# Spectral filter and max-out MLP on one core: who doubles the filter in the opening, and evacuations of two PSUM banks

## Chip, cores, metric

The kernel runs on one core of a Trainium2 chip. The metric is the device time of one execution in microseconds (us). The engines are TensorE (matmul), VectorE, ScalarE, GpSimd and SyncE; in the profile they are PE (with PEld for weight loads), DVE, ACT, POOL and SP. Transfers are issued by SyncE (the hardware queue, q1) and by GpSimd (the software queue, q0).

## The reference

A batch of 8 sequences of 3072 tokens with 256 channels is filtered along the sequence in the frequency domain; the result, taken as 24576 tokens, goes through an MLP that takes the larger of two projections.

```python
X = np.fft.rfft(x, axis=1)                      # x: 8 x 3072 x 256
Y = X * (filt_r + 1j * filt_i)[None]            # filter: 1537 x 256
y = np.fft.irfft(Y, n=3072, axis=1).astype(np.float32)
t = y.reshape(24576, 256)
out = np.maximum(t @ w1, t @ w2) @ w_out        # w1, w2: 256 x 1024, w_out: 1024 x 256
```

## The kernel before

**Algorithm.** The length 3072 is split as 96 x 32, and the transforms are matmuls against tables that the kernel makes itself: `C1` (forward, 96 points), `U` (forward, 32 points with the twiddle factors), `VP` and `VQ` (the way back over 32 points), `G1` (back over 96 points). Between forward and back lies the product with the filter `F`. The max-out uses max(a, b) = b + relu(a - b): `Wd` is w1 - w2, `M` is w2 times w_out, and a token block is relu(y Wd) Wo + y M.

**Steps of a batch.** `s1` (or `f1`) multiplies x by the 96-point table; `s2` multiplies by `U` and leaves `px` in PSUM, two tiles for each `v` (s = 0, 1); `product` multiplies `px` by `F` into `pq`, real and imaginary filter at once (128 partitions x 1024 elements); `s3` multiplies by `VP` and `VQ`; `s4` makes the time signal from `zr`; `moe_h` and `moe_o` are the MLP. `v` runs over 6 groups, each of 2 of the 12 filter windows `w`. From the second batch on these steps are spread over 64 steps of the MLP of the batch before, by the lists at the end of the kernel. That steady loop takes up most of the time.

**The opening** is the first batch, which has no MLP beside it. It is written out by hand (L562 to L651), under a manual schedule: each engine runs its instructions in the order in which the code gives them. [...] `spin` issues matmuls on a constant whose result is not used.

**The filter.** `F` holds each value on two groups of 32 partitions (0 to 31 and 32 to 63, and the same from 64). `load_f` brings it from memory into the first of each with transfers of GpSimd that also convert to bfloat16: for windows 0 to 7 and then 8 to 11, and in each for two partition halves `g` and two parts `ri`, rows upward (L117) and rows backward (L120). `double_f` copies it to the second group: windows 0 to 7 by four VectorE copies (L130), windows 8 to 11 by four transfers of SyncE (L132), behind which SyncE issues the loads of w1 and w2 (L281, L282). `fix_f` sets one row.

**Who multiplies.** VectorE makes the s = 0 products of all six groups. The s = 1 products of groups 0, 2, 3 and 4 are GpSimd's (`POOLED`), that of group 1 VectorE's, and that of group 5 is shared, half and half (`shared_product`, L388 and L389). GpSimd's queue is: loads of x, the issues of `F`, a load of the second batch (`load_x(1, 0, 2)`, L172), its products, two further x loads, `Wd` first half, the load of `Wo`, an x load, `Wd` second half, `CT`.

**PSUM.** Two pools hold the 8 banks from the start: `ps` (6 tiles of one bank) and `pso` (2). A tile waits until the buffer it takes has been read.

**Order of rows.** `U`, `bt` and `zT` are indexed by `u = 2 * w + g` (w = 2v + i), and `kc` and `kap`, from which the tables come, count in that order.

Of the kernel before, what the change touches and what calls it, by code (L numbers as in the profile page):

```python
# [26 lines left out]
def kernel(  # L27
# [40 lines left out]
    ps = ctx.enter_context(tc.tile_pool(name="ps", bufs=6, space=bass.MemoryType.PSUM))  # L68
    pso = ctx.enter_context(tc.tile_pool(name="pso", bufs=2, space=bass.MemoryType.PSUM))
# [3 lines left out]
    pq0 = setup.enter_context(tc.tile_pool(name="pq0", bufs=6))  # L73
    ctx.enter_context(tc.manual_schedule())
# [35 lines left out]
    def load_f(h):  # L110
        w0, w1 = WP[h]
        n = 2 * (w1 - w0)
        for g in range(2):
            for ri, f in enumerate((filt_r, filt_i)):
                k0 = 24 * g + 2 * w0
                src = bass.AP(f.tensor, f.offset + k0 * D, [[96 * D, 16], [D, n], [1, D]])
                G.dma_start(out=F[64 * g:64 * g + 16, ri, w0:w1].rearrange("p w s d -> p (w s) d"), in_=src)  # L117
                n0 = 1 if k0 == 0 else 0
                src = bass.AP(f.tensor, f.offset + (96 - k0 - n0) * D, [[96 * D, 16], [-D, n - n0], [1, D]])
                G.dma_start(out=F[64 * g + 16:64 * g + 32, ri, w0:w1].rearrange("p w s d -> p (w s) d")[:, n0:n],  # L120
                            in_=src)
                if n0:
                    src = bass.AP(f.tensor, f.offset + 48 * D, [[96 * D, 16], [1, D]])
                    G.dma_start(out=F[16:32, ri, 0, 0], in_=src)

    def double_f(h, g, ri, engine):
        w0, w1 = WP[h]
        o_, i_ = F[64 * g + 32:64 * g + 64, ri, w0:w1], F[64 * g:64 * g + 32, ri, w0:w1]
        if engine is V:
            V.tensor_copy(o_, i_)  # L130
        else:
            nc.sync.dma_start(out=o_, in_=i_)  # L132
# [9 lines left out]

    V.memset(W1, 1.0)
# [3 lines left out]
    kc = init.tile([NP, NW, 2, 2], FP32)  # L147
    kap = init.tile([128, NW, 2], FP32)
# [3 lines left out]
    hv = init.tile([128, 2, 1], FP32)  # L152
    load_x(0, 0, 1)
    G.iota(pid, pattern=[[1, 1]], base=0, channel_multiplier=1, allow_small_or_imprecise_dtypes=True)
    G.iota(kc, pattern=[[2, NW], [24, 2], [1, 2]], base=0, channel_multiplier=0,
           allow_small_or_imprecise_dtypes=True)
    load_x(0, 1, 1)
    G.iota(kap, pattern=[[2, NW], [24, 2]], base=0, channel_multiplier=0,
# [4 lines left out]
    for c in range(3, 8):  # L163
        load_x(0, c, 1)
    for q in range(2):
        G.memset(hv[:, q], 1.0)
        for r in (0, 32):
            G.memset(hv[r:r + 1, q], 0.5 * (1 - q))
    load_f(0)
    load_f(1)  # L170
    load_fn()
    load_x(1, 0, 2)  # L172

    def table_c():
# [4 lines left out]
        kf = kc.rearrange("p w g s -> p (w g s)")  # L179
# [16 lines left out]
    def tables_u():  # L196
# [24 lines left out]
        V.tensor_scalar(t1[:, 0], kap.rearrange("p w g -> p (w g)"), a_, base, OP.mult, OP.add)  # L221
# [19 lines left out]
    def sines_u(h):  # L241
        uv = ua.rearrange("p u c s j -> p u (c s j)")
        S.activation(U[:, NW * h:NW * h + NW], uv[:, NW * h:NW * h + NW], AF.Sin, bias=zero, scale=TWO_PI)

    def table_g():
        pg = ps.tile([96, NP], FP32, tag="ps", name="pg")
# [3 lines left out]
    def table_v(h, q):  # L250
        pool, tag = (pso, "po") if h else (ps, "ps")
        pv = [pool.tile([128, 6, 64], FP32, tag=tag, name="pv%d" % s) for s in range(2)]
        for i in range(6):
            for g in range(2):
                for s in range(2):
                    rows = slice(64 * s, 64 * s + 64)
                    u = 2 * (6 * h + i) + g
                    if q == 0:
                        TE.matmul(pv[s][64 * g:64 * g + 64, i], U[rows, u], I128[rows, rows], start=True, stop=True)
                    else:  # L260
                        TE.matmul(pv[s][64 * g:64 * g + 32, i], U[rows, u, 32:64], I128[rows, rows],
                                  start=True, stop=True)
                        TE.matmul(pv[s][64 * g + 32:64 * g + 64, i], U[rows, u, 0:32], NI[rows, rows],
# [3 lines left out]
    def put_v(h, q, pv):  # L267
        for s in range(2):
            i0 = 1 if h == 0 and s == 0 else 0
            tab = VQ if q else VP  # L270
            if i0:
                S.activation(tab[:, 0, 0], pv[0][:, 0], AF.Identity, bias=zero, scale=hv[:, q])
            S.activation(tab[:, 6 * h + i0:6 * h + 6, s], pv[s][:, i0:6], AF.Copy)  # L273
# [97 lines left out]
    def s2(b, v):  # L371
        px = [ps.tile([128, 2, D], FP32, tag="ps", name="px%d" % s) for s in range(2)]
        for i in range(2):
            for s, g in ((0, 0), (1, 1), (0, 1), (1, 0)):
                u = 2 * (2 * v + i) + g
# [4 lines left out]
    def product(E, v, s, px, pool=None):  # L380
# [3 lines left out]
        return pq  # L384

    def shared_product(v, s, px, xs_, pool):
        pq = pool.tile([128, 2, 2, D], BF16, tag="pq", name="pq")
        V.tensor_tensor(pq[:, 0], px, F[:, 0, 2 * v:2 * v + 2, s], OP.mult)  # L388
        G.tensor_tensor(pq[:, 1], xs_, F[:, 1, 2 * v:2 * v + 2, s], OP.mult)  # L389
        return pq  # L390

    def s3(b, v, pq):
# [9 lines left out]
        for g in range(2):  # L402
            S.activation(zt[:, :, g], pz[g], AF.Copy)  # L403
        nc.sync.dma_start(out=zd[b][4 * v:4 * v + 4].rearrange("u p d -> p u d"),
                          in_=zt.rearrange("p i g d -> p (i g) d"))
# [89 lines left out]
    def s1t(c):  # L495
        for dc in range(2):
            pa = ps.tile([128, 4, 96], FP32, tag="ps", name="pa")
            for m in range(4):
                TE.matmul(pa[:, m], xb[0, c][:, m, 128 * dc:128 * dc + 128], C1, start=True, stop=True)
            o_ = at2[:, dc].rearrange("p u q m -> p (u q) m")[:, :, 4 * c:4 * c + 4]  # L500
            i_ = pa.rearrange("p m q -> p q m")
            if dc == 1 and c >= 6:
# [237 lines left out]
```

## Time and profile before

| what | value |
|---|---|
| median of 3 runs | 503.91 us (503.34 to 505.15) |
| the profiled execution's own time | 503.8 us |
| its span (first to last instruction) | 502.0 us |
| mean granted TensorE clock | 0.992 |
| TensorE busy | 488.4 us, 97% |
| VectorE, ScalarE, GpSimd busy | 331.9, 308.3, 257.5 us |
| four doublings on VectorE (L130) | 1217 ns each |
| ScalarE evacuations in `s1t` (L505) | 14 of 487 ns |
| products on VectorE and on GpSimd in the opening (L382) | 7 of 1217 ns, 4 of 2130 ns |

A row of a timeline gives the start in us from the span's start, the busy time, the engine, the line of the kernel, the operation, what it writes and reads, how many there are, and in brackets how long the engine stood idle before it and what ended that. The chain of waits is followed back from the last instruction to what released each piece. Issues of transfers are listed with size and time to landing, from the start of the issue.

### The profile page before, as it was taken

The page shows a single profiled execution, that of the slowest core. Times are in us where ns is not written, and L with a number is a line of the kernel's source. Part 1 is how long each engine was busy: PE and PEld are TensorE (multiplying, and loading weights), DVE is VectorE, ACT ScalarE, POOL GpSimd, SP SyncE. Part 2 cuts the span into 40 slices and gives each one's busy share as a digit, 9 for nine tenths or more (in the row PEclk, how much of TensorE's full clock was granted, in tenths as well). Part 3 has the DMA queues.
Part 4 walks back from the last instruction along what each step waited for, and adds up shares of the span by engine and source line. Part 5 has one row for each costly group of instructions (what it writes and reads, how often), then busy time and mean ns, then how long its engine had stood idle before and what let it go on. Part 6 is the DMA issues. An engine that isn't in the chain of part 4 may idle for free.

```text
span 502.0 us, 13079 instructions
## 1 busy us (share of the span) xinstructions
PE 488.4 (97%) x5299; PEld 362.1 (72%) x5303; DVE 331.9 (66%) x518; ACT 308.3 (61%) x629; POOL 257.5 (51%) x338
## 2 busy tenths in 40 slices
PE   8688999999999999999999999999999999999997
PEld 3455777777777777777777777777777777777775
DVE  7876688457865777457765687557765687555553
ACT  6776478647774676557764586647774465544442
POOL 7893569547463864645654855537632221222220
PEclk9989999999999999999999999999999999999999
DMA  7999789995799667986779558896769235411112
GB/s 125 150 252 217 230 229 290 306 274 171 212 268 260 175 204 234 250 229 189 198 244 275 187 177 245 235 239 197 197 181 255 78 111 153 168 65 64 64 64 84
DMA packets 77966, 97.20 MB, mean 194 GB/s; under 512 B 8017, under 2 KB 54354, under 8 KB 77842
## 3 DMA queue, kind: packets, MB, share of 16 engines
q1 hardware_dynamic: 64642, 66.73, 49.6%
q0 software_dynamic: 13264, 29.64, 20.3%
q8 instruction: 41, 0.67, 0.6%
q14 instruction: 19, 0.16, 0.1%
HBM read 53.87 MB, written 47.19 MB: 201 GB/s over the span
## 4 chain that ended last, share of the span: by engine, by line
PE 90%; DMA 5%; POOL 2%; issue 1%; ACT 1%; DVE 0%; SPq 0%; POOLq 0%; DVEq 0%
PE po L476 34%; PE ph L448 33%; PE po L474 8%; PE pz L399 5%; PE py L428 4%; PE pa L349 2%; DMA F<-in_filt_r_dram 2%; PE px L376 2%; DMA Wo<-in_moe_w_out_dram 2%; POOL xb L88 1%; DMA F<-F 1%; PE pr L549 1%; POOL pq L382 0%; PE pt L528 0%; PE pm__1132 L306 0%
## 5 line engine op out<-in xcount | busy, mean ns | idle before, releaser
L476 PE MATMUL po<-Wo,gt 128*128 128x256 bf16 x1536 | 261.0, 273 | 0.2 <-DMA Wo<-in_moe_w_out_dram 0.2
L452 ACT ACTIVATE gt<-ph 128x384 bf16<-128x384 f32 x321 | 157.0, 496 | 147.9 <-PE ph L448 147.3
L461 POOL DMA_DIRECT2D out_dram<-ot x186 | 102.6, 555 | 187.1 <-DVE ot L488 184.4
L476 PEld LDWEIGHTS <-gt 128*128 128x128 bf16 x1536 | 146.6, 98 | 66.1 <-issue 10.3
L450 DVE TENSOR_SCALAR gt<-ph 128x384 bf16<-128x384 f32 x191 | 104.9, 552 | 63.1 <-PE ph L448 59.9
L382 DVE TENSOR_TENSOR pq<-px,F 128x1024 bf16<-128x1024 f32 x91 | 107.0, 1219 | 24.2 <-PE px L376 22.6
L448 PEld LDWEIGHTS <-Wd 128*128 128x128 bf16 x1024 | 96.5, 98 | 12.9 <-POOL Wd L292 1.4
L103 POOL TENSOR_TENSOR xb<-XF 128x512 bf16<-128x512 f32 x48 | 61.2, 1276 | 41.3 <-DMA XF<-in_x_dram 21.2
L488 DVE COPY ot<-po 128x512 f32<-128x512 f32 x95 | 65.1, 685 | 25.3 <-PE po L476 25.0
L104 POOL TENSOR_TENSOR xb<-XF 128x512 bf16<-128x512 f32 x48 | 61.0, 1271 | 0.0
L403 ACT ACTIVATE zt<-pz 128x512 bf16<-128x512 f32 x84 | 45.6, 595 | 11.5 <-PE pz L399 8.4
L353 ACT ACTIVATE at<-pa 128x512 bf16<-128x512 f32 x96 | 51.8, 610 | 1.2 <-PE pa L349 0.8
L428 PE MATMUL py<-G,zr 96*128 96x96 bf16 x512 | 32.7, 206 | 0.2
L428 PEld LDWEIGHTS <-zr 96*128 96x128 bf16 x512 | 29.0, 97 | 2.5 <-DVE zr L552 0.4
L399 PE MATMUL pz<-pq,VP 64*64 64x256 bf16 x336 | 21.9, 281 | 0.0
L376 PE MATMUL px<-bt,U 64*64 64x256 bf16 x384 | 19.8, 278 | 1.2 <-ACT VQ L273 0.7
L399 PE MATMUL pz<-pq,VQ 64*64 64x256 bf16 x336 | 20.9, 269 | 0.0
L349 PE MATMUL pa<-xb,CT 64*64 64x512 bf16 x192 | 19.5, 383 | 0.0
L399 PEld LDWEIGHTS <-VP 64*64 64x64 bf16 x336 | 9.7, 105 | 13.3 <-issue 13.3
L376 PEld LDWEIGHTS <-U 64*64 64x64 bf16 x384 | 10.4, 109 | 3.9 <-issue 3.3
L559 PE MATMUL pd<-W 128*128 128x512 bf16 x30 | 10.5, 462 | 1.7 <-DVE zero L145 1.5
L552 DVE COPY zr<-pr 96x1024 bf16<-96x1024 bf16 (+1 forms) x8 | 5.2, 649 | 8.0 <-PE pr L549 8.0
(429 smaller groups left out, 609.7 us busy)
## 6 DMA issues: line engine op xcount, KB each, us to landing
out_dram<-ot POOLq DMA_DIRECT2D x186, 128.0 KB, 3.3
XF<-in_x_dram SPq DMA_DIRECT2D x96, 192.0 KB, 4.6
ad<-at SPq DMA_DIRECT2D x56, 192.0 KB, 3.3
bt<-ad SPq DMA_DIRECT2D x14, 768.0 KB, 9.1
zd<-zt SPq DMA_DIRECT2D x42, 256.0 KB, 2.7
zr<-zd SPq DMA_DIRECT2D x56, 192.0 KB, 4.8
WS<-in_moe_w_dram SPq DMA_DIRECT2D x4, 512.0 KB, 5.1
xb<-in_x_dram POOLq DMA_DIRECT2D x8, 192.0 KB, 5.8
```

What stands on the lines that cost most here:

```text
L103: G.tensor_tensor(t_[:, 0], f[:, 0], f[:, 1], OP.add)
L104: G.tensor_tensor(t_[:, 1], f[:, 0], f[:, 1], OP.subtract)
L353: S.activation(at[:, m0:m0 + 2], pa[g], AF.Copy)
L382: E.tensor_tensor(pq, px.rearrange("p (o i) d -> p o i d", o=1).to_broadcast([128, 2, 2, D]), F[:, :, 2 * v:2 * v + 2, s], OP.mult)
L399: TE.matmul(pz[g][64 * s:64 * s + 64, i], tab[64 * g:64 * g + 64, 2 * v + i, s], pq[s][64 * g:64 * g + 64, q, i], start=(q == 0), stop=(q ...
L428: TE.matmul(py[:, m], zr[b][:, 4 * i + m, 128 * dc:128 * dc + 128], G1, start=True, stop=True)
L448: TE.matmul(ph, Wd[:, dc, 128 * j:128 * j + 128], y_[:, dc], start=(dc == 0), stop=(dc == 1))
L450: V.tensor_scalar(gt[tt][:, j], ph, 0.0, None, OP.max)
L452: S.activation(gt[tt][:, j], ph, AF.Relu)
L461: E.dma_start(out=dst, in_=ot[tt // 2][:, 3 * (tt % 2) + c])
L476: TE.matmul(p_, g_[:, n - 2, blk], Wo[:, n - 2], start=(e == 0), stop=(e == 9))
L488: V.tensor_copy(ot[tt // 2][:, e - 1:e + 1], po[0])
```

## The change

- `double_f` works on three parts of four windows. VectorE copies windows 0 to 3 (groups v = 0, 1); SyncE copies windows 4 to 7 and then 8 to 11, eight transfers of the same size as the four before.
- `load_f` is called by direction: for windows 0 to 7 the four upward loads, then the backward ones, then the same for windows 8 to 11. The transfers are the same eighteen.
- Until the end of the opening, PSUM is held by `pair` (2 tiles of two banks) and `single` (4 tiles of one bank); `ps` and `pso` are opened after it. ScalarE evacuates both banks of a pair in one instruction: in `s1t` for c < 7, in `put_v`, and in `s3t` for v < 5. In the last call of `s1t` and of `s3t`, ScalarE and VectorE take one bank each.
- The order of rows becomes `u = 4 * v + 2 * g + i`; `kc`, `kap`, `s2`, `table_v`, `zT` and (in the steady loop too) the block order inside `zt` follow it.
- The factor 0.5 or 0 for the first row moves from an evacuation with a scale (L272) into `U0`, one VectorE multiplication with `hv`, for which GpSimd makes 3 memsets instead of 6.
- `sines_u(0)` follows c = 3 instead of 4, `sines_u(1)` follows the last `s1t`; `put_v`, `s2`, `products` and `s3t` are reordered; GpSimd gets the s = 1 products of groups 0 to 3, VectorE those of 4 and 5; `load_x(1, 0, 2)` is issued behind the first product; `s3t` has one constant matmul ahead for every v.

```diff
-    ps = ctx.enter_context(tc.tile_pool(name="ps", bufs=6, space=bass.MemoryType.PSUM))
-    pso = ctx.enter_context(tc.tile_pool(name="pso", bufs=2, space=bass.MemoryType.PSUM))
+    pair = setup.enter_context(tc.tile_pool(name="pair", bufs=2, space=bass.MemoryType.PSUM))
+    single = setup.enter_context(tc.tile_pool(name="single", bufs=4, space=bass.MemoryType.PSUM))
...
-    def load_f(h):
+    def load_f(h, sign):
...
+                r0 = 64 * g if sign > 0 else 64 * g + 16
+                o_ = F[r0:r0 + 16, ri, w0:w1].rearrange("p w s d -> p (w s) d")
+                if sign > 0:
+                    src = bass.AP(f.tensor, f.offset + k0 * D, [[96 * D, 16], [D, n], [1, D]])
+                    G.dma_start(out=o_, in_=src)
+                else:
+                    src = bass.AP(f.tensor, f.offset + (96 - k0 - n0) * D, [[96 * D, 16], [-D, n - n0], [1, D]])
+                    G.dma_start(out=o_[:, n0:n], in_=src)
...
     def double_f(h, g, ri, engine):
-        w0, w1 = WP[h]
-        o_, i_ = F[64 * g + 32:64 * g + 64, ri, w0:w1], F[64 * g:64 * g + 32, ri, w0:w1]
+        ws = slice(4 * h, 4 * h + 4)
+        o_, i_ = F[64 * g + 32:64 * g + 64, ri, ws], F[64 * g:64 * g + 32, ri, ws]
...
-    load_f(0)
-    load_f(1)
+    for h in range(2):
+        load_f(h, 1)
+        load_f(h, -1)
     load_fn()
-    load_x(1, 0, 2)
...
     def put_v(h, q, pv):
-        for s in range(2):
-            i0 = 1 if h == 0 and s == 0 else 0
-            tab = VQ if q else VP
-            if i0:
-                S.activation(tab[:, 0, 0], pv[0][:, 0], AF.Identity, bias=zero, scale=hv[:, q])
-            S.activation(tab[:, 6 * h + i0:6 * h + 6, s], pv[s][:, i0:6], AF.Copy)
+        S.activation((VQ if q else VP)[:, 6 * h:6 * h + 6].rearrange("p i s m -> p s i m"), pv, AF.Copy)
...
     def s1t(c):
+        pa = two("pa") if c < 7 else None
...
+        if c < 7:
+            S.activation(o_, pa.rearrange("p c m q -> p c q m"), AF.Copy)
+        else:
+            S.activation(o_[:, 0], pa[0].rearrange("p m q -> p q m"), AF.Copy)
+            V.tensor_copy(o_[:, 1], pa[1].rearrange("p m q -> p q m"))
...
     def s3t(v, pq):
...
+        zv = zT[:, :, :, 4 * v:4 * v + 4].rearrange("p c m u q -> p u (c m) q")
+        if v < 5:
+            S.activation(zv, t_.rearrange("p g (i q n) -> p (g i) n q", i=2, q=4), AF.Copy)
+        else:
+            S.activation(zv[:, 0:2], pz[0].rearrange("p i s r c m -> p i (c m) (s r)"), AF.Copy)
+            V.tensor_copy(zv[:, 2:4], pz[1].rearrange("p i s r c m -> p i (c m) (s r)"))
...
-    for g in range(2):
-        for ri in range(2):
-            double_f(1, g, ri, nc.sync)
+    for h in (1, 2):
+        for g in range(2):
+            for ri in range(2):
+                double_f(h, g, ri, nc.sync)
...
-    POOLED = (0, 2, 3, 4)
+    POOLED = (0, 1, 2, 3)
...
-    pxs = {v: s2(0, v) for v in (1, 0)}
-    stage_x(0)
...
+    pxs = {v: s2(0, v) for v in (0, 1)}
+    for v in range(2):
+        stage_x(v)
+    for q in range(2):
+        put_v(0, q, table_v(0, q))
+    for v in range(2):
+        pqs[v] = products(v)
+        if v == 0:
+            load_x(1, 0, 2)
+        pxs[v + 2] = s2(0, v + 2)
+        stage_x(v + 2)
+        put_v(1, v, table_v(1, v))
+    s3t(0, pqs[0])
+    pqs[2] = products(2)
+    pxs[4] = s2(0, 4)
+    pqs[3] = products(3)
     s3t(1, pqs[1])
...
     for v in (4, 5):
         pqs[v] = products(v)
-    for v in (4, 5):
+    for v in (2, 4, 3, 5):
         s3t(v, pqs[v])
...
+    ps = ctx.enter_context(tc.tile_pool(name="ps", bufs=6, space=bass.MemoryType.PSUM))
+    pso = ctx.enter_context(tc.tile_pool(name="pso", bufs=2, space=bass.MemoryType.PSUM))
```

## The prediction

> **What bounds the kernel now.** I read the page first: engines, 40 slices, chain. TensorE is busy 97% of the span and the chain is 90% TensorE; the rest of the chain (transfers, GpSimd, 10%) lies in the opening. The edits to the steady loop change the order of filter rows in `u` and the place of blocks inside `zt`, not one size or count, so I cost the loop at nothing: its instructions would keep their rows (84 evacuations of 595 ns at L403). The change can only move the moment from which TensorE is fed without a gap. That moment I looked up in the chain of waits in order of time (start, length, what):
>
> ```profile
> PE 90%; DMA 5%; POOL 2%; issue 1%; ACT 1%; DVE 0%; SPq 0%; POOLq 0%; DVEq 0%
> ...
> 16.69 4.13 DMA F<-in_filt_r_dram
> ...
> 21.61 3.23 DMA F<-F
> ...
> 30.64 2.10 POOL pq L382
> 32.73 1.15 POOL pq L389
> ...
> 37.19 9.41 DMA Wo<-in_moe_w_out_dram
> 46.60 0.04 issue
> 46.64 0.60 PE po L476 x4
> ```
>
> From 46.64 on it is TensorE nearly throughout. Before that it is the filter: loaded by GpSimd, doubled over the partitions, multiplied on GpSimd. The timelines of VectorE and GpSimd show how tightly these sit (start, busy, line, idle before):
>
> ```profile
> 18.15 1.22 DVE L130 COPY F<-F 32x4096 bf16<-32x4096 bf16 x1
> 19.40 0.28 DVE L140 CAST F<-FN 1x256 bf16<-1x256 f32 x1
> 19.72 3.60 DVE L130 COPY F<-F 32x4096 bf16<-32x4096 bf16 x3
> 23.82 5.75 DVE L382 TENSOR_TENSOR pq<-px,F 128x1024 bf16<-128x1024 f32 x5 [0.50 <-DVE F L130]
> 30.60 2.36 DVE L382 TENSOR_TENSOR pq<-px,F 128x1024 bf16<-128x1024 f32 x2 [1.03 <-DMA F<-F]
> 32.87 0.68 DVE L388 TENSOR_TENSOR pq<-px,F 128x512 bf16<-128x512 f32 x1
> ```
> ```profile
> 17.69 0.53 POOL L120 DMA_DIRECT2D F<-in_filt_i_dram  x1
> 18.22 1.25 POOL L117 DMA_DIRECT2D F<-in_filt_r_dram  x1
> 19.57 1.49 POOL L120 DMA_DIRECT2D F<-in_filt_r_dram  x1
> 21.05 1.24 POOL L117 DMA_DIRECT2D F<-in_filt_i_dram  x1
> 22.28 1.17 POOL L120 DMA_DIRECT2D F<-in_filt_i_dram  x1
> 23.43 0.52 POOL L88 DMA_DIRECT2D xb<-in_x_dram  x1
> ```
>
> Two things are to be seen. While VectorE runs its four copies, each filter issue on GpSimd takes 1.2 to 1.5 us instead of 0.5, one issue per copy, so the last leaves at 22.28. And VectorE then stands 1.03 us until 30.60 for SyncE's last transfer (issued 26.45, landed 30.45). After it come 3.4 us: two and a half products on VectorE, in parallel one and a half on GpSimd, which ends at 33.88. The last `zT` is written at 35.19, TensorE's transposes start at 35.34. I call the end of the last product E (33.88) and the landing of SyncE's last doubling T (30.45).
>
> **The change, part by part.** *VectorE's doubling* shrinks from four copies of 4096 elements to four of 2048. Half of 1.217 us is 0.61; a copy of 1024 elements takes 0.69 over 128 partitions (L516), so 0.6 to 0.7. Four and the 0.28 fix make 2.7 to 3.1 us in place of 5.2, and the first products start near 21.5 instead of 23.82. This gains nothing by itself: groups 4 and 5 cannot be multiplied before T.
>
> *Filter issues.* Eighteen before and after. Each waits for the landing of the one eight places earlier (GpSimd's waits at 9.92 to 14.11 are for the x loads), so the last waits for the tenth filter load, landed at 20.2. It leaves between 20.2 and, if nothing is relieved, 22.28. With one shorter copy per issue I take 20.8.
>
> *Landing of that load.* Before: 4.1 us (22.28 to 26.4). Up to 21 us the DMA engines are full (share 1.09 from 15 to 20 us), then the late issues leave holes. SyncE's four additional transfers, those of windows 4 to 7, fall into this stretch. Two such transfers in the stretch 21.5 to 24.5 took 27.2% of 3 us of all engines, 0.4 each, so four put 1.6 us of work ahead of the last loads. Bounds for the landing: 20.2 + 3.5 = 23.7 (if they cost nothing; 3.4 is the shortest such load) and 26.4; I take 24.8.
>
> *SyncE's last transfer* then issues at 24.9 instead of 26.45. Its price is the main unknown. The four of before took from issue to landing:
>
> ```profile
> F<-F SPq DMA_DIRECT2D x1, 128.0 KB, 2.9
> F<-F SPq DMA_DIRECT2D x1, 128.0 KB, 3.2
> F<-F SPq DMA_DIRECT2D x1, 128.0 KB, 5.4
> F<-F SPq DMA_DIRECT2D x1, 128.0 KB, 4.0
> ```
>
> The 5.4 was issued at 23.56, 0.13 us behind the 384 KB load of the next batch (`load_x(1, 0, 2)`, GpSimd, 23.43, landed 5.3 us later). What the engines moved while it hung shows why:
>
> ```profile
> q0 software_dynamic: 216, 0.39, 99.9%
> q1 hardware_dynamic: 4, 0.02, 1.6%
> ```
>
> This is 24.5 to 27.2 us: GpSimd's queue has nearly all, SyncE's nearly nothing. In the new order that load stands behind GpSimd's first product: start about 21.6, plus 2.13, so it is issued near 23.8, again about a microsecond ahead of SyncE's last transfer. I take 4.9, near the 5.4; bounds 2.9 and 5.4. T = 24.9 + 4.9 = 29.8.
>
> *Behind T.* Before, VectorE and GpSimd shared groups 4 and 5. Now GpSimd has groups 0 to 3 (four of 2.13 us and an issue of 0.52 from 21.6: done near 30.7) and VectorE all four products of groups 4 and 5: with the pitch of 1.17 (7 in 5.75 + 2.36) that is 4.7, with 0.15 of wake-up 4.85 against 3.43. E = 29.8 + 4.85 = 34.65, 0.75 later. Break-even is T = 29.0. VectorE is idle from about 27 to T, so nothing else on it matters.
>
> *ScalarE's pairs.* Seven 768-wide evacuations for fourteen of 487 ns (four back to back took 1.60, 0.40 each); four in `put_v`, five 1024-wide in `s3t`. A pair costs between 0.80 and the 0.94 of the 768-wide sine, a `zT` pair about 1.02 (L514) for 1.09. In `s1t` the x loads hide it (TensorE's weight loads wait 4.1 us for them); uncovered it would be 7 x 0.14 = 1.0 us. Later ScalarE waits 2.3 us for `s3t` anyway.
>
> *Without a price on the path.* `sines_u(1)` (0.94) moves into ScalarE's 1.34 us gap at 16.09; TensorE's wait of 1.54 for it goes, but the next tables now wait for VectorE's first product, which frees `px` (four single banks instead of six), near 22.7; uncovered 1.3 us, covered as GpSimd has products 0 and 1 to do until 26. `U0` (0.35 by L228) lies in VectorE's gap of 0.59 at 14.43. Three fewer memsets save GpSimd 0.4, which waits for x loads at once. The moved x load would land near 29.2 and is needed at 34.37 (L324). SyncE's weight loads stand behind eight transfers instead of four but leave at about 25.5 instead of 27.01. `s3t(4)`'s cast goes from VectorE (0.68) to ScalarE.
>
> *Behind E.* GpSimd reaches `Wd` near 32 instead of 34.90, `Wo` leaves 3 us earlier. TensorE's 0.67 for the second half of `Wd` and 0.18 for `Wo` go. But VectorE is busy 4.90 of 5 us from 40 to 45, and TensorE waits 0.70 there for its `w2b`: the 0.67 only moves into that wait. I count 0.2. Sum: +0.75 - 0.2 = about +0.5 on the profiled 503.8 (span 502.0 and 1.8 around it; the median is 503.91): **504.3 us**.
>
> **Rivals.** *1. SyncE's eight transfers become the bound: slower.* Place: T. If the added 1.6 us and the 384 KB load count in full, the last filter load lands at 25.5 and the transfer takes 5.4: T = 31.0, E = 35.85, +2.0 - 0.2: 505.6. It decides from T = 30.75. For it: the 5.4 row. Against: the first two transfers, 2.9 and 3.2.
>
> *2. SyncE's transfer isn't held up: faster.* If it takes 2.9 to 3.2 and the last load lands at 24.0 to 24.4, T is 27.0 to 27.6, E 31.85 to 32.45, and with the 0.2 that is -1.6 to -2.2: 501.6 to 502.2. For it: two of four rows; against it the 1.6% above. [...]
>
> *3. The half clock.* TensorE was busy 1.19 of 3.41 us from 20.44 to 23.85 and then ran at 0.50 until 30.68; with 2.53 of 3.41 (17.02 to 20.44) it kept 1.0. I expect about 2.4 of 3.41 ahead of 34 us. If the clock falls there, `s3t` takes 1.0 (26.37 to 27.40) instead of 0.55, and with transposes, `s4` and the first `moe_h` about 1.0 is added: 505.3. [...]
>
> *4. The issues aren't relieved.* Last issue at 22.28, T = 30.45 as before, E +1.4: 505.0.
>
> **How the numbers follow.** Measurements of this kernel tell 0.3% from no change, so "same" is 502.4 to 505.4. Forecast 0.37 (all same), rival 1 0.24 (slower), rival 2 0.21 (faster), rival 3 0.12 (two thirds slower, as it may come on top of a late T), rival 4 0.06 (half and half). That is 0.21 faster, 0.44 same, 0.35 slower. The forecast alone spans 503.0 to 505.3 (T from 28.8 to 30.7). The range reaches into both rivals of T, 501.8 to 506.2.
>
> **What would show it.** Filter issues of 0.5 to 0.7 us after 18 us, the last by 21; VectorE's first L382 near 21.5, then an idle stretch that ends with a DMA F<-F at 29 to 30.5; the last product at 34 to 35. Wrong: a last F<-F before 28 or after 31, GpSimd's fourth product later than VectorE's last, or a TensorE gap behind 47 us that was not there.

## The result, and the profile after

The changed kernel takes **510.65 us** (median of 6 runs, 509.17 to 512.01), the kernel before in the same job 504.47 us (6 runs, 502.87 to 505.22): ratio **1.0124**, 95% interval 1.0098 to 1.0149. The prediction was 504.3 with a range to 506.2; it is wrong by 6.3 us, well outside the range. The profiled execution after took 510.68 us, its span is 508.9. From the first `po` to the end both kernels take the same (455.4 and 455.7 us), so all of the difference lies in the opening. The chain of waits says where (start, length, what):

```profile
PE 90%; DMA 5%; DVE 2%; POOL 1%; issue 0%; SPq 0%; ACT 0%; DVEq 0%; POOLq 0%
...
20.71 5.75 DMA F<-in_filt_r_dram
...
28.41 4.86 DMA F<-F
...
38.97 1.01 PE pz L538 x32
39.98 0.02 issue
40.01 0.70 DVE zT L546
40.71 0.04 issue
40.76 0.66 PE pa L332
...
53.40 0.44 PE po L481 x4
```

It is the same chain as before, filter load, doubling, products, `zT`, and each link is later. In the opening, `s1t` multiplies x by `C1` and evacuates into `at2`, `t1` transposes into `bt`, `table_v` and `put_v` make `VP` and `VQ` for 6 windows at a time, `stage_x` has ScalarE copy the s = 1 half of `px` to `xs`, which GpSimd's products read (`pq<-xs,F`, all 5 of them before and all 4 after), `s3t` takes `pq` to `zT`, and `t2` transposes that into `zr`. The timelines of VectorE and of GpSimd after (start, busy, line, idle before):

```profile
19.47 0.68 DVE L134 COPY F<-F 32x2048 bf16<-32x2048 bf16 x1 [0.94 <-DMA F<-in_filt_r_dram]
...
21.08 2.07 DVE L134 COPY F<-F 32x2048 bf16<-32x2048 bf16 x3 [0.62 <-DMA F<-in_filt_i_dram]
23.26 2.35 DVE L393 TENSOR_TENSOR pq<-px,F 128x1024 bf16<-128x1024 f32 x2
27.72 2.36 DVE L393 TENSOR_TENSOR pq<-px,F 128x1024 bf16<-128x1024 f32 x2 [2.10 <-DMA F<-F]
33.69 4.62 DVE L393 TENSOR_TENSOR pq<-px,F 128x1024 bf16<-128x1024 f32 x4 [3.61 <-DMA F<-F]
40.01 0.69 DVE L546 CAST zT<-pz 128x512 bf16<-128x512 f32 x1 [1.70 <-PE pz L538]
```
```profile
19.29 0.96 POOL L121 DMA_DIRECT2D F<-in_filt_r_dram  x1 [0.55 <-DMA F<-in_filt_r_dram]
...
22.69 0.59 POOL L124 DMA_DIRECT2D F<-in_filt_i_dram  x1
23.31 2.12 POOL L393 TENSOR_TENSOR pq<-xs,F 128x1024 bf16<-128x1024 f32 x1
25.38 0.57 POOL L88 DMA_DIRECT2D xb<-in_x_dram  x1
...
35.61 2.35 POOL L300 TENSOR_TENSOR Wd<-WS 128x1024 bf16<-128x1024 f32 x1 [2.33 <-DMA WS<-in_moe_w_dram]
...
43.66 2.34 POOL L300 TENSOR_TENSOR Wd<-WS 128x1024 bf16<-128x1024 f32 x1 [4.32 <-DMA WS<-in_moe_w_dram]
```

Three things are to be seen. VectorE's copies are short, as costed, but the first ones now wait for filter loads. VectorE waits twice for doublings, 2.10 and 3.61 us. GpSimd's filter issues are short again (0.48 to 0.96 us from 19.29 on) but wait for the landings of earlier ones (0.55 us ahead of 19.29), and later it waits for the expert weights. By stages, with T the start of VectorE's first product of group 4 and E the end of the last product of all (the prediction's T, the landing of SyncE's last doubling ahead of that start, was 30.45 before and is 33.27 now):

| us from the span's start | before | after | later by |
|---|---|---|---|
| T | 30.60 | 33.69 | 3.1 |
| E | 33.88 | 38.31 | 4.4 (1.3 of it behind T) |
| last `zT` written | 35.19 | 40.70 | 5.5 |
| first matmul of `s4` | 36.25 | 43.34 | 7.1 |
| Wd, second half, starts on GpSimd | 38.65 | 43.66 | 5.0 |
| first `po` | 46.64 | 53.23 | 6.6 |

So three stretches lose: 3.1 up to T, 1.3 from T to E, 2.2 from E to `po`. The experiments take them in turn, first with one part of the change alone in the kernel before, then with one part undone in the changed kernel, then in sums. Each time is a median; a ratio is to the kernel before on the same chip, with its 95% interval.

### The profile page after: what moved, and what is told of

It reads as the page before. It is cut to its first block, busy times and chain, and to the rows that moved or that the text cites. A ratio compares the mean times of both kernels' runs of the same rounds, so it can differ in the third digit from the quotient of the medians.

```text
span 508.9 us, 13067 instructions
## 1 busy us (share of the span) xinstructions
PE 492.5 (97%) x5302; PEld 364.7 (72%) x5302; DVE 329.6 (65%) x517; ACT 307.6 (60%) x612; POOL 253.7 (50%) x334
## 4 chain that ended last, share of the span: by engine, by line
PE 90%; DMA 5%; DVE 2%; POOL 1%; issue 0%; SPq 0%; ACT 0%; DVEq 0%; POOLq 0%
PE po L481 34%; PE ph L453 32%; PE po L479 8%; PE pz L404 5%; PE py L433 4%; DMA F<-in_filt_r_dram 3%; PE pa L357 2%; PE px L387 2%; DMA xb<-in_x_dram 1%; DMA F<-F 1%; PE pr L557 1%; PE pz L538 1%; DVE at L335 0%; DVE pq L393 0%; PE pa L332 0%; POOL xb L88 0%
## 5 line engine op out<-in xcount | busy, mean ns | idle before, releaser
L393 DVE TENSOR_TENSOR pq<-px,F 128x1024 bf16<-128x1024 f32 x92 | 108.3, 1219 | 28.5 <-PE px L387 22.6
L567 PE MATMUL pd<-W 128*128 128x512 bf16 x31 | 12.0, 507 | 1.5 <-DVE zero L156 1.5
```

Source lines behind the costliest of these rows:

```text
L393: E.tensor_tensor(pq, px.rearrange("p (o i) d -> p o i d", o=1).to_broadcast([128, 2, 2, D]), F[:, :, 2 * v:2 * v + 2, s], OP.mult)
```

## Experiments: one part alone in the kernel before

**e3, the order of the loads alone.**

```diff
-    load_f(0)
-    load_f(1)
+    for h in range(2):
+        load_f(h, 1)
+        load_f(h, -1)
```

> The kernel before with nothing changed but the order of the filter loads (by direction). Theory O: packets of the backward loads take twice as long, the last doubling lands 2 us or more later than 30.45, and the time is 506.5 to 509. Theory S: within 0.3% of before, 503 to 505.5.

Measured: 507.43 us, 1.0070 (1.0046 to 1.0094); T at 33.98, 3.4 later than before, and `po` at 49.68, 3.0 later. A step that issues the same eighteen transfers costs more than half of what the whole change does. The order changes how fast they run. In the row for 15 to 20 us (busy times of the engines, clock, then the DMA share and GB/s) of the kernel before, and then of e3, the share rises from 1.09 to 1.65 while less is moved:

```profile
15.00:20.00 5.00, 4.10 (x92) 3.47 (x92) 3.86 (x6) 3.91 (x7) 4.60 (x8) 1.00 1.09 160
```
```profile
15.00:20.00 5.00, 4.07 (x92) 3.39 (x89) 3.15 (x5) 3.63 (x6) 3.25 (x6) 1.00 1.65 131
```

In the trace's single packets (software queue, the 1536 of 512 bytes and the 64 of 8 KB) a 512-byte packet of a backward load takes 66 ns on average before and 95 in e3, an 8 KB packet of an upward load 643 and 746. In the changed kernel it is 105 and 816, with a share of 1.74 at 120 GB/s.

**e9, the same order of directions, but halves alternating.** In the new order two loads in a row (real, imaginary) write the same 16 partitions; before, each load (but for two small ones of 8 KB) wrote other ones than the load ahead of it. Here the loop over the halves `g` goes inside, in `load_f` and in both doublings:

```diff
-        for g in range(2):
-            for ri, f in enumerate((filt_r, filt_i)):
+        for ri, f in enumerate((filt_r, filt_i)):
+            for g in range(2):
```

> The kernel before, with the filter loads issued by direction as in the changed kernel (all upward ones of four windows, then all backward ones), but changing the half of the partitions from load to load, where the changed kernel (and the earlier run of the order alone, 507.4) puts two loads in a row into the same 16 partitions. The doublings follow in the same order. If two in a row into the same partitions are what slows the packets, upward packets are back at about 0.06 us and 0.62 us per load, VectorE's products of group 4 start near 31 and the time is 504 to 505. If the run of one direction itself does it, the packets stay at 0.1 us and more, the products start near 34 and the time is 507 to 508, as in the run of the order alone.

Measured: 504.77 us, 1.0020 (1.0003 to 1.0037); T 30.98. The packets are back at 66 and 624 ns, and the row for 15 to 20 us too:

```profile
15.00:20.00 5.00, 4.07 (x93) 3.40 (x89) 3.70 (x5) 3.62 (x6) 4.46 (x8) 1.00 1.12 151
```

So not the run of one direction but which loads stand next to each other costs most of it: 0.50 of the 0.70%. That the target partitions are the reason, and not something else that the swap of the two loops changes (the order of the two sources, or of the doublings), is inferred: e3 and e9 are two orders of the same loads, and no run changes the partitions alone.

**e4, SyncE's eight transfers alone** (loads in the old order).

```diff
-        w0, w1 = WP[h]
+        ws = slice(4 * h, 4 * h + 4)
...
-    for g in range(2):
+    for h in (1, 2):
+        for g in range(2):
```

> The kernel before with nothing changed but the doubling: VectorE windows 0 to 3, SyncE 4 to 7 and 8 to 11 in eight transfers. Theory O: at most 1 us later, 503.5 to 505.5, or a little faster, as GpSimd's issues are no longer held up. Theory S: last doubling after 32, 506.5 to 509.

Measured: 504.74 us, 1.0017 (1.0004 to 1.0029); T 31.83. This is the cleanest test of the prediction's first steps. The chain of waits of e4:

```profile
20.50 5.72 DMA F<-in_filt_i_dram
26.22 0.02 SPq L132
26.24 0.03 issue
26.27 5.13 DMA F<-F
```

The last filter issue does come 1.8 us earlier (20.50 for 22.28), as forecast (20.8). But its load takes 5.7 us instead of 4.1 and lands at 26.22, where it landed before (26.4). What the relieved issue gives is lost in the load, which shares the engines with the four further transfers (89.5% for GpSimd's queue and 29.9% for SyncE's from 21 to 22 us); that they are what slows it is the likely reason, not isolated. Then the doubling takes 5.1, where it took 4.0.

**e10, the x load later, alone.** The 384 KB load of the next batch moves behind GpSimd's second product (28.45 instead of 23.43).

```diff
     load_fn()
-    load_x(1, 0, 2)
...
     for v in (1, 0, 2):
         pqs[v] = products(v)
+    load_x(1, 0, 2)
```

> The kernel before with the 384 KB load of the next batch (load_x(1, 0, 2)) issued behind GpSimd's second product, near 28.2, instead of ahead of all products at 23.43. Nothing else. If that load is what holds SyncE's third doubling (5.4 us against 2.9 and 3.2), the third and fourth take about 3 us each, the products of group 4 start near 29.3 instead of 30.6, and the time falls by 0.6 to 1.2 to about 503, with the load landed near 32.5, ahead of its use at 34.4. If the doublings are slow because of the last filter loads themselves, their durations stay at 4 to 5 us, the start stays within 0.3 of 30.6 and the time within 0.4 of before, or above it by what the first f1 then waits for the load.

Measured: 505.27 us, 1.0019 (1.0003 to 1.0035). The transfers did what was expected, the time did not. SyncE's last two doublings (issues with size and time to landing) take 3.7 and 2.2 us where before they took 5.4 and 4.0:

```profile
F<-F SPq DMA_DIRECT2D x1, 128.0 KB, 3.7
...
F<-F SPq DMA_DIRECT2D x1, 128.0 KB, 2.2
```

VectorE then runs its seven products from 24.61 to 32.62 without a stop. But GpSimd, with the load between its products, still ends at 34.37, and the load, now behind the weights, lands 7.8 us after its issue: TensorE's first f1 waits 1.4 us for it and `s4` starts at 38.90 instead of 36.25. The x load does hold the doublings up, and neither of the two places tried here is free.

## Experiments: one part undone in the changed kernel

**e1, loads in the old order; e2, doubling as before (VectorE windows 0 to 7, SyncE 8 to 11).**

```diff
-        load_f(h, 1)
-        load_f(h, -1)
+        load_f(h)
```
```diff
-        ws = slice(4 * h, 4 * h + 4)
+        ws = slice(*WP[h])
...
-    for h in (1, 2):
-        for g in range(2):
-            for ri in range(2):
-                double_f(h, g, ri, nc.sync)
+    for g in range(2):
+        for ri in range(2):
+            double_f(1, g, ri, nc.sync)
```

> The changed kernel with the filter loads in the order of before (upward, then backward, for each half and part). Theory O (loading by direction slows the transfers themselves: 512-byte packets of the backward loads took up to 0.15 us instead of 0.06): the last filter load lands by 25.5 us, SyncE's last doubling near 30, the last product ends near 35, and the time is 504.5 to 506.5. Theory S (the four added SyncE transfers are what delays the filter): the last doubling still lands after 32.5 and the time stays at 509 to 511.

> The changed kernel with the doubling of before (VectorE copies windows 0 to 7, SyncE 8 to 11), loads still by direction. Theory O: the backward loads still land last and late, SyncE's last doubling lands after 31.5, and the time stays at 508 to 511. Theory S: the last doubling lands by 30.5 and the time falls to 505 to 507.

Measured: e1 509.10 us, 1.0100 (1.0083 to 1.0117), T 32.86; e2 508.72 us, 1.0089 (1.0059 to 1.0118), T 33.33. Either alone takes back only 0.24 and 0.35 of the 1.24%: T stays late, since the other cause holds it.

**e5, e1 with the x load right behind the filter loads; e13, the order by direction with halves alternating (as e9), in the changed kernel.**

```diff
     load_fn()
+    load_x(1, 0, 2)
...
-        if v == 0:
-            load_x(1, 0, 2)
```

> The changed kernel with two parts undone: filter loads in the order of before, and the second batch's first x load issued right behind the filter loads, ahead of GpSimd's first product. Theory X (with the order undone, what still holds up SyncE's last transfer is the x load issued about a microsecond ahead of it): the last doubling lands near 30 instead of 32.7 and the time falls by 1.5 to 3 from 509.1, to 506 to 507.5. Rival (it is SyncE's own eight transfers and not the x load): T stays above 32 and the time within 0.7 of 509.1.

> The changed kernel with the same loads by direction, but changing the half of the partitions from load to load (the loop over the real and imaginary filter outside, the halves inside), and the doublings in the same order. In the kernel before this alone took away nearly all of what the new order costs (507.43 with two loads in a row into the same 16 partitions, 504.77 so). If it does the same here, the DMA share from 15 to 20 us falls from 1.74 to about 1.1, VectorE's products of group 4 start by 32 instead of 33.69 and the time falls by 1.5 to 3, to 507.5 to 509. If the eight transfers of SyncE take the same time whatever the loads, the start stays above 33 and the time above 509.5.

Measured: e5 508.71 us, 1.0091 (1.0067 to 1.0115), but T falls to 30.07, better than before. e13 510.15 us, 1.0114 (1.0089 to 1.0140), T only 33.16. In e13 the loads are fast again (packets 66 and 624 ns, share 1.17), GpSimd issues the last by 21.65, the first products start at 21.11. VectorE then shows where it went:

```profile
24.90 2.35 DVE L393 TENSOR_TENSOR pq<-px,F 128x1024 bf16<-128x1024 f32 x2 [1.44 <-DMA F<-F]
33.16 4.62 DVE L393 TENSOR_TENSOR pq<-px,F 128x1024 bf16<-128x1024 f32 x4 [5.90 <-DMA F<-F]
```

SyncE issues its last four doublings from 24.05 to 26.26. The first of their packets moves at 27.55, when 81 of the 96 packets of the x load (issued at 23.73) have gone; the last lands at 32.74. What the queues moved from 25.3 to 27.7 us in e13:

```profile
q0 software_dynamic: 74, 0.30, 73.7%
q1 hardware_dynamic: 1, 0.00, 0.4%
```

These shares count a packet where it starts. In rows of one microsecond the DMA share of e13 is 1.26, 0.78 and 1.04 from 25 to 28 us, 3.08 us of packets in 3, so the engines may have been full; what held SyncE's packets is open.

So two causes lie behind T, the neighbours among the loads and the x load ahead of the doublings, and each hides the other. In e5 both are gone and T is early, yet the time stays: the weights, issued from 26.7, land late, and TensorE waits 1.4 us for Wd's second half. From the chain of e5:

```profile
29.13 12.91 DMA WS<-in_moe_w_dram
...
42.18 2.35 POOL Wd L296
```

**e6, TensorE kept busy.** Constant matmuls: 10 ahead of the tables of half 1, and 3 and 16 instead of one in `s3t(1)` and `s3t(4)`.

```diff
-        TE.matmul(pz[0].rearrange("p i s r c m -> p (i s r c m)"), W1[:, 0:128], W1, start=True, stop=True)
+        for _ in range({1: 3, 4: 16}.get(v, 1)):
+            TE.matmul(pz[0].rearrange("p i s r c m -> p (i s r c m)"), W1[:, 0:128], W1, start=True, stop=True)
```

> The changed kernel with constant matmuls added in places where TensorE stands waiting (10 ahead of one table_v, 3 ahead of s3t(1), 16 ahead of s3t(4)), so that its clock does not fall. Theory C (the half clock from 24 to 45 us costs what lies between the last product and the first moe_h, 6.5 us here against 3.6 before): granted clock 1.0 again by 35 us, products at the same times, the time 1.8 to 2.8 lower, near 508.3. Rival (the slow matmuls are hidden, the loss is all in T and the products): within 0.7 of 510.6.

Measured: 509.41 us, 1.0109 (1.0086 to 1.0132). The changed kernel runs at half clock from 23.9 to 44.4 us (before: 22.7 to 29.6). In its row for 30.94 to 34.36 (PE busy first, then PEld, VectorE, ScalarE, GpSimd, clock) TensorE is busy 1.87 us, at 0.50; the same row of e6, with 3.13 us at 1.00, follows:

```profile
30.94:34.36 3.42, 1.87 (x34) 0.98 (x33) 0.67 (x1) 1.02 (x1) 2.33 (x3) 0.50 0.96 310
```
```profile
30.94:34.36 3.42, 3.13 (x14) 1.21 (x13) 0.00 (x0) 0.63 (x1) 2.08 (x3) 1.00 0.99 292
```

At full clock to 37 us (then 0.50 once more, to 40.4), E to `po` shrinks from 14.92 to 13.56. What was regained of the clock is worth about 1.3 us here, less than the 1.8 to 2.8 expected and near the 1.0 of the prediction's third rival.

**e7, the old division of the products** (GpSimd 0, 2, 3, 4 and half of 5; `s3t` in order).

```diff
-    POOLED = (0, 1, 2, 3)
+    POOLED = (0, 2, 3, 4)
...
+        if v == 5:
+            pq.append(shared_product(v, 1, pxs[v][1], xs[v], pool))
...
-    for v in (2, 4, 3, 5):
+    for v in (2, 3, 4, 5):
```

> The changed kernel with the division of products of before (VectorE both of group 1, GpSimd's share in groups 4 and 5) and s3t in the order 2, 3, 4, 5. T stays at 33.4. Theory P (four VectorE products behind T cost 1.4 us more than the divided work): the last product ends near 36.8 instead of 38.3, the time 1.3 to 2.5 lower, 508 to 509.3. Rival (the products are not on the path): within 0.7 of 510.6.

Measured: 509.74 us, 1.0120 (1.0098 to 1.0142). T to E shrinks from 4.62 to 3.25, and next to nothing of that reaches the end, where 1.3 to 2.5 us had been expected.

**e11, transposes first; e14, with it the x loads behind Wd's first half.**

```diff
+    t2(0, (V, S))
     f1(1, 0, S)
     spin(1)
-    t2(0, (V, S))
-    spin(2)
```
```diff
+    prep_wd(0, G)
     for c in (2, 4):
         load_x(1, c, 2)
-    prep_wd(0, G)
```

> The changed kernel with the transposes of the last stage (t2) put ahead of the first f1 and its spin, and without the two spins behind it. In the changed kernel the PSUM pools of the loop are opened only where the opening's are closed, so the first f1 waits for the last read of the opening's banks, and it and a spin stand ahead of the transposes: 2.64 us from the last zT to the first matmul of s4, where before it was 1.06. If this is a term of its own, the 2.64 shrinks to 1.5 to 2.0 and the time falls by 0.4 to 0.9, to 509.5 to 510.3. If the half clock alone makes the 2.64, it stays above 2.3 and the time within 0.3 of the changed kernel.

> The changed kernel with the transposes ahead of the first f1 (as in the run before, which took 1.5 us out of the gap behind the last zT and nothing out of the time), and GpSimd's two x loads of 384 KB moved behind the first half of Wd. In that run GpSimd waited 4.37 us for the last expert weights, which took 12.2 us to land next to those x loads. If the weights are the second chain that swallowed the gain, the last of them now lands in 5 to 7 us, Wd's second half starts by 41 instead of 44.74, the first po by 51.3, and the time is 508.5 to 509.7. If not, Wd may move but po and the time stay (510.3 to 511).

Measured: e11 510.63 us, 1.0126 (1.0113 to 1.0139); e14 509.66 us, 1.0114 (1.0077 to 1.0151). In e11 the stretch from the last `zT` to `s4` falls from 2.64 to 1.11, further than expected, and the time does not move; the stretch runs at full clock here (from 39.1 on) and at half clock in the changed kernel, so part of the 1.5 us is the clock's. The chain of e11 has left the filter:

```profile
32.39 12.20 DMA WS<-in_moe_w_dram
...
44.74 2.35 POOL Wd L300
```

The last weights leave SyncE at 32.39 behind eight doublings (before: 29.36 behind four) and run into GpSimd's x loads of 32.89: 12.2 us. Wd, `moe_h` and `po` wait for them. In e14 Wd's second half starts at 41.37, `po` only moves from 52.35 to 52.34 (T was 1.1 later in that run), and the gain of e14 against e11, 0.12%, is within the intervals. That the weights carry the end in e11 is shown by its chain; what they cost is not settled.

## Experiments: sums, and single parts put back

**e8, e1 with the early x load and the old division; e12, with it transposes first and constant matmuls (6, and 3, 2 and 8 in three `s3t`); e15, loads by direction and eight transfers kept, but halves alternating, early x, old division, transposes first, x loads behind Wd.** Their edits are those shown.

> The changed kernel with the order of the loads, the place of the x load and the division of products as before; what is left of the change is the doubling by three parts, the pairs of banks, U0, the moved sines and the reordered opening. If orders, x load and division account for the whole loss: 503 to 505.5, the same as before. If the pairs or the rest of the reordering cost something of their own: above 506.

> The changed kernel with the four suspected losses taken out at once: filter loads in the old order, load_x(1, 0, 2) right behind them, the old division of the products, transposes first; and constant matmuls put in (6 ahead of the tables of half 1, 3, 2 and 8 in three of the s3t stages) to keep TensorE's clock up. Three of these together gave 505.67, 1.003 of before. If what is left there (2.6 us from the last zT to s4, first half at half clock) is all that still separates the kernels, this gives 503 to 504.5, equal to before or better, with s4 about 1.1 to 1.6 us behind the last zT and moe_h's first matmul 1.2 us behind that. If the eight transfers of SyncE still cost on top, it stays at 505 or above.

> The changed kernel with VectorE's and SyncE's new division of the doubling and the loads by direction kept, but: halves alternating, load_x(1, 0, 2) right behind the filter loads, the old division of the products, transposes first, x loads behind the first half of Wd. If loads in a row into the same partitions, the place of the x load, the division, the pool's wait and the late weights are the whole loss, this comes to 504.5 to 506 (with about 0.9 left for the eight transfers, as in before). If something of the new order stays, 507 or above.

Measured: e8 505.67 us, 1.0030 (1.0015 to 1.0046); e12 505.37 us, 1.0017 (1.0007 to 1.0028); e15 506.93 us, 1.0048 (1.0028 to 1.0068); e8 and e15 lie between the two cases that were expected of each. Alone the old division gave 0.04% (e7) and the x load's place 0.09% (e1 to e5); together they give 0.70% (e1 to e8). I read this as chains that end at the same time and have to be cut all at once.

The record shows one such chain that no list of single parts has. With the new division GpSimd is through with its products by 30.6 to 33.0 us and then issues its x loads, while SyncE's last weight load, late behind eight doublings, is under way. In the six such runs (the changed kernel, e1, e5, e6, e11, e13) that load takes 10.7 to 12.9 us; in the six with eight doublings where those x loads come later (e4, e7, e8, e12, e14, e15) it takes 6.9 to 9.0. How much of the time this is stays open: the profiled executions of e5 (507.20, its shortest) and e8 (507.80, its longest) have their first `po` at 49.80 and 49.58.

e12 is where eight transfers alone (e4) stand. In e15 the order by direction still costs: all four last doublings wait for backward loads at the very end, of which one, issued at 21.64 beside the early x load, takes 6.9 us; they leave SyncE by 29.0 and T is 32.13.

**e16, everything of the opening undone but the pairs** (e8 with e2's doubling and transposes first): old loads, old doubling, old division, early x; kept are ScalarE's pairs, the tables' order, `sines_u(1)` early and the late PSUM pools.

> What of the change is then left: old order of the loads, VectorE's doubling of four groups and SyncE's of two as before, x load behind the filter loads, old division of the products, transposes first; kept are ScalarE's evacuations of two banks at once, the tables in the order of the pairs, sines_u(1) early and the PSUM pools opened late. If the eight transfers are what still separates the runs with three and four parts undone (505.67, 505.37) from before (504.2), this equals before: 503.8 to 504.8. If the pairs and the late pools cost by themselves, it stays at 505 or above. If the pairs help, it is below 503.5.

Measured: 504.29 us, 1.0000 (0.9986 to 1.0013). ScalarE's part costs nothing and brings nothing, to within 0.14%.

**e17, e16 with the new division of the products; e18, e16 with the first f1 ahead of the transposes.** Their edits are those of e7 and of e11, backward.

> The kernel of the run before (equal to before: 504.29, ratio 1.000; of the change only the pairs, the tables' order and the late pools kept) with one thing of the change put back: the division of the products, GpSimd groups 0 to 3, VectorE all of groups 4 and 5, and s3t in the order 2, 4, 3, 5. The prediction's step: 4.85 us behind the landing of the last doubling instead of 3.43, so +1.4. If that holds by itself, VectorE's last product ends 4.6 us behind its start of group 4 and the time is 505.2 to 506. If VectorE, with three products fewer before, reaches groups 4 and 5 earlier than the shared order did, it stays at 503.8 to 504.8.

> The same kernel with the first f1 and its spin ahead of the transposes again, as in the changed kernel. There its matmul waits for the last read of the opening's banks, because the pools of the loop are opened only then. If that is a price of its own where no weights are late, the gap from the last zT to the first matmul of s4 grows from 1.1 to 1.5 or more (2.64 at half clock) and the time by 0.4 to 1.0, to 504.7 to 505.3. If not, the time stays within 0.3 of 504.3.

Measured: e17 504.57 us, 1.0011 (0.9995 to 1.0026), less than expected; e18 505.30 us, 1.0023 (1.0007 to 1.0038), at the upper end. In e17 VectorE's last product ends 4.62 behind its start, 1.3 us later than before, but GpSimd, without products behind T, starts Wd's halves 1.5 us earlier than before (33.40 and 37.18). In e18 TensorE's matmul of f1 waits for the last read of the opening's banks, and transposes and `s4` stand behind it (start, busy, line):

```profile
37.30 0.66 PE L328 MATMUL pa<-xb,C 96*96 96x512 bf16 x1 [0.81 <-DVE zT L548]
37.76 0.63 PE L569 MATMUL pd<-W 128*128 128x512 bf16 x1
38.18 1.06 PE L559 MATMUL pr<-I,zT 128*96 128x128 bf16 x8
39.03 1.06 PE L569 MATMUL pd<-W 128*128 128x512 bf16 x2
39.89 0.67 PE L435 MATMUL py<-G,zr 96*128 96x96 bf16 x8
```

This stretch lies wholly in half clock (0.50 from 36.81 to 40.23), which set in before the first instruction that e18 moves. So the 0.23% is not the pools' alone. The mean granted clock of each execution says how much of it was at half clock, though not where. In e18 the six at 0.992 or more have a median of 504.53, the six below 506.04; in e16 such halves have 504.20 and 504.53, in e9 (seven and five) 503.98 and 506.68. So f1 behind the pools costs some 0.3 us where little time is at half clock and 1.5 where more is; the 0.20% of e9, too, goes along with the clock.

**The account.** Put in one at a time where nothing else is late, the parts cost: order of the loads 0.70% (e3), eight transfers 0.17% (e4), first f1 behind the pools 0.23% (e18 against e16), division 0.11% (e17 against e16, not distinguishable from nothing), pairs 0.00% (e16). Together 1.21%; the change measures 1.24% (0.98 to 1.49). Each term is uncertain by about 0.13 to 0.25% and averages over runs with more and with less time at half clock, so the agreement is partly luck; and the x load's place and the late weights, which act only beside the others, are not in it. Added up for other runs, the terms come near e8 (0.40 for 0.30) and e12 (0.17 for 0.17), but not e5 (0.51 for 0.91): they do not simply add. No version ran faster than the kernel before; e16 is level with it.

## Why the prediction was wrong

- **VectorE's copies and the first products.** 3.03 us for the four copies and the fix (forecast 2.7 to 3.1). The first products started at 23.26, not near 21.5: the copies waited 0.94 and 0.62 for loads. With halves alternating (e13) it is 21.11.
- **Filter issues, "I take 20.8".** Right with the loads in the old order (20.50 in e4), wrong for the changed kernel (22.69). The wait that the step names, for the landing eight places earlier, is in both traces: an issue that waits starts 0.28 us behind that landing (before, 15.66 behind 15.37; after, 19.29 behind 19.02). Before, the last two filter issues started 1.57 and 2.15 us behind it, each right behind another issue of 1.2 to 1.5 us, beside VectorE's copies; in the changed kernel the last three started 0.28 behind it, and those landings were late (the last of them at 22.41, for 20.13 before). So rival 4's late issue came, by another cause, and not its T of 30.45.
- **The step that failed first: "Landing of that load ... I take 24.8", with bounds of 23.7 and 26.4.** The last backward load landed at 27.8. I took the eighteen loads as the same work in another order and gave the order no price and no rival; in the kernel before it moves the landing from 26.4 to 28.1 and the start of group 4 by 3.4 us (e3); with halves alternating the packets are back at 66 and 624 ns and group 4 starts at 30.98 (e9). Even in the old order the load landed at 26.2 (e4), at my upper bound: the load then took 5.7 us for 4.1, nearly as much as the earlier issue gained.
- **"SyncE's last transfer ... I take 4.9".** Right: 4.86, issued at 28.41 instead of 24.9. The x load ahead of it does hold it up (with that load later, the last two doublings take 3.7 and 2.2 us for 5.4 and 4.0, e10). The landing that it calls T was 33.3, not 29.8, and so past the sign of being wrong that the prediction names (after 31); of the 3.5 us, 3.0 came from the landing of the load and 0.5 from four doublings that became ready together and left 0.6 apart.
- **"Behind T ... 4.85".** It was 5.04: 4.62 for the products (forecast 4.7) and 0.42 from the landing to the first of them (0.15). But the step took E's delay as the time's delay; of the 1.3 us in e17 the median shows 0.11%, about 0.6 us, at the end (interval -0.3 to 1.3).
- **"Behind E ... I count 0.2".** This term failed second: 2.2 lost instead of 0.2 gained. The late opening of `ps` was not costed at all; with f1 ahead of the transposes it takes about 1.2 us in the median of e18, part of it the clock's. The weights, said to leave at 25.5, left at 29.0 to 31.3, the last took 12.2 us, and GpSimd, which was to reach `Wd` near 32 and reached it at 33.3, waited 2.33 and 4.32 us for them. The half clock, costed as a rival at 1.0, came on top (e6: 1.3). Its windows were read 1.1 us late: before, the clock was 0.50 from 22.7 to 29.6, and TensorE was busy 1.45 of the 3.41 us ahead of the fall, not 1.19.
- **ScalarE's pairs and the rest at nothing.** Right (e16).
- **The rivals.** Rival 1 had the right place, SyncE's transfers as the bound from T = 30.75 on, but a T of 31.0 at most, because it too let the loads run as before; e4, the eight transfers alone in the kernel before, has that landing at 31.4. Rival 2's condition, a transfer that is not held up, was met in e10 (last landing at 27.5) and gave no time, since GpSimd's products still ended at 34.37. In e13 SyncE's packets had 0.4% of the engines' time beside the 73.7% of GpSimd's queue, which speaks against this rival unless they were not yet there to be moved; the trace does not show when they were.

## What to carry to other kernels

The order of transfers had a cost here: eighteen loads in another order made the time 0.70% longer (e3), and 0.20% with halves alternating (e9). Before loads are regrouped, see which partitions neighbours write (here the likely reason, not isolated), and which consumers then all become ready with the last load (in the changed kernel four doublings, which left 0.6 us apart). Where several chains end close to each other, undoing one part may show little (e7: 0.04%, where with others it was part of 0.70%); put the parts one at a time into the kernel before, where nothing else is late. And a pool of PSUM opened late put its first user behind the last reader of the pool before (`pa` waited 0.81 us for `zT` in the changed kernel and in e18), with the transposes behind it on TensorE.

## What was not expected of the hardware

- A 512-byte packet took 66 ns on average or 95, and an 8 KB packet 624 or 746, by the order of loads alone (e9 against e3); in the changed kernel 105 and 816, with halves alternating (e13) 66 and 624. In the five other runs with the changed kernel's order of loads it was 82 to 108 and 710 to 794.
- Four 128 KB transfers of the hardware queue, issued from 24.05 to 26.26, moved nothing until 27.55 while a 384 KB load of the software queue ran (e13). With that load later, such transfers took 3.7 and 2.2 us in all (e10).
- The stretches at a clock of 0.5 in the opening lasted 6.83 us before and 20.48 in the changed kernel, two and six times 3.41. In the changed kernel the clock stayed at 0.5 through five windows of 3.41 us, in which TensorE was busy between 1.82 and 2.94 us, and came back only after one that it filled (40.95 to 44.36, 3.41 of 3.41). It was not so in e11, where it came back after one with 2.70 of 3.41 (35.73 to 39.14). With constant matmuls it stayed at 1.0 to 37 us instead of 23.9 (e6), for 1.3 us of gain.
